# Gated linear attention and a multiplicative feed-forward on one core: masked scores in quarters, with a second load of v for the odd heads

## The chip, the cores and the metric

One core of a Trainium2 chip runs the whole program. The metric is the device time of one execution in microseconds (us); a kernel is compared by the median of its runs on the same chip. The profile is one execution, recorded by the hardware profiler.

## The reference

```python
# attention, for every one of B=4 batches and H=8 heads; S=768 tokens, D=48
state = alpha[:, :, t, :, None] * state + einsum('bhd,bhe->bhde', k[:, :, t], v[:, :, t])
y[:, :, t] = einsum('bhd,bhde->bhe', q[:, :, t], state)
# y is laid out as x: 3072 tokens x 384, then
a = x @ w1; b = x @ w2            # 384 x 1024 each
out = ((a * b) @ w3) @ w_out      # 1024 x 1024, 1024 x 384
```

Within a chunk of 128 tokens the recurrence is computed as masked attention: with q and k scaled by running products of alpha, a query t sees the keys s <= t of its chunk through a 128 x 128 matrix of scores, and everything earlier through the 48 x 48 state. Of the four 64 x 64 quarters of a score matrix one, later keys with earlier queries, is all masked.

## The kernel before, in words

**Stages.** Part 1 is a loop over N = 24 chunks (6 to a batch) of all 8 heads, into which the first gate products of the feed-forward are mixed as filler. After it come the remaining gate products, the folding of w3 with w_out, and the last projection.

**A chunk's work.** Heads go in pairs j = 0..3 with i = 0 for the even and i = 1 for the odd head; head i of a pair lies on partitions 64i to 64i+47 of `qkT`. For chunk n the pieces are:

- `load_a`, `load_kq`, `load_v`: alpha, k and q, v from memory on SP's queue, all in rows of 48 numbers (192 bytes). `load_v` (L151) writes one of four buffers `vs`.
- `logs`, `decays`, `decayed` (L288 on): Ln on ScalarE (ACT), the running sums on TensorE (L318 to L324), two Exp into a tile `e` (L326, three buffers), and the product with k and q on VectorE (DVE, L337). For every even chunk that doesn't open a batch, single rows of `e` go through memory by POOL's queue (L330, L332, L345) to become the state's decay `dec`.
- `transposed` (L348): 16 transposes into PSUM (L359), two copies to `qkT` on ACT (L361).
- `scores` (L393): 8 float32 matmuls, each of 48 rows by 128 keys as weights with 128 queries moving, the even and the odd head in two row halves of the array (L399); then two VectorE instructions that AND the 128 x 512 scores of four heads with an integer mask `keep` into the tile `ms` (L402).
- `attend_state` (L408): 8 matmuls of state with q into two PSUM banks `y`, in four 64 x 64 corners of the array (L419).
- `attend` (L422): 8 matmuls with 64 columns of v as weights and 128 columns of `ms` moving, onto the same banks (L425), in two column halves; then two copies on ACT (L429), which `store` sends to memory as `xd` (L283) one iteration later.
- `outer`, `advance`: the chunk's own k by v (L371), added to the state on VectorE (L379, L381), decayed on POOL (L390).

**The order.** Iteration n of the loop is written out by hand:

```python
store(); ...load_x, load_a(n + 5); load_kq(n + 4); load_v(n + 2)
attend_state(n - 1)
scores(n)
transposed(n + 1)
...split_x, convert
advance(n); attend(n - 1); outer(n)
...run(pieces), decayed(n + 2), logs(n + 4), decays(n + 3), convert
```

So the masks of chunk n are made in iteration n and used by `attend(n)` in iteration n+1, behind that iteration's scores and transposes. Each engine takes its instructions in one order, and SP's queue issues its DMAs in one order; a scheduler that orders a program's instructions may move one ahead of others of its engine that are not ready. The trace of before shows TensorE in the order above, and SP in it until about 140 us. From iteration 6 on `run(pieces)` adds up to three pieces of gate products (`exact`, L455), 9 matmuls of 384 columns each, to an iteration; in one iteration of four (9, 13, 17, 21) there is none. `convert` turns the float64 weights into float32 parts, mostly VectorE and ACT work, with loads `raw` of 512 KB on SP (L213).

Of the kernel before, what the change touches and what calls it, by code (L numbers as in the profile page):

```python
# [10 lines left out]
FP32 = mybir.dt.float32  # L11
FP32R = mybir.dt.float32r
I32 = mybir.dt.int32
# [3 lines left out]
ALU = mybir.AluOpType  # L17
# [31 lines left out]
def kernel(  # L49
# [12 lines left out]
    nc = tc.nc  # L62
    B, H, S, D = q.shape
    C = 128
    DM = H * D
    DF = moe_w1.shape[1]
    NCH = S // C
    N = B * NCH
    NP = H // 2
    DP = 64  # L70
# [6 lines left out]
    AHEAD = 3  # L77
    LATE = 10
    PAIRED = 8
    assert D <= DP and DM % C == 0 and DF % CW == 0 and S % C == 0 and N % G == 0  # L80
    assert DM <= 512 and TG <= 512

# [17 lines left out]
    p1 = pool("p1", 1, stack=part1, side="right", reuse_waits="tile")  # L100
# [3 lines left out]
    def bank():  # L104
        return ps.tile([C, 512], FP32, tag="bank", name="bank")

    st, mark = {}, {}
# [14 lines left out]
    vs = [p1.tile([C, H, DP], FP32, name=f"v{i}") for i in range(AHEAD + 1)]  # L122
    for x in vs:
        nc.gpsimd.memset(x[:, :, D:], 0.0)

    def rows(src, n):
        b, c = divmod(n, NCH)
        return src[b, :, ds(c * C, C), :].rearrange("h p d -> p h d")
# [22 lines left out]
    def load_v(n):  # L151
        if n < N:
            st["v", n] = vs[n % len(vs)]
            (nc.gpsimd if 2 < n < 8 else nc.sync).dma_start(out=st["v", n][:, :, 0:D], in_=rows(v, n))

    spare = tr[0].tile([C, 3 * KM * TG], FP32R, tag="x3", name="x3")[:].bitcast(FP32)
    sums2 = spare[:, 0:4 * C].rearrange("p (e s t) -> p e s t", e=2, s=2)
    pairs = [spare[:, ds(4 * C + i * 2 * DM, 2 * DM)].rearrange("p (h s d) -> p h s d", h=H, s=2) for i in range(2)]
# [18 lines left out]
    sums = p1.tile([C, 2, C], FP32R, name="sums")  # L177
    signs = p1.tile([C, 2, C], FP32R, name="signs")
    keep = p1.tile([C, C], I32, name="keep")
    qks = [p1.tile([C, 2, H, DP], FP32, name=f"qk{i}") for i in range(3)]  # L180
    Ts = [p1.tile([C, NP, DP], FP32, name=f"T{i}") for i in range(2)]
    decs = [p1.tile([C, 3, NP], FP32, name=f"dec{i}") for i in range(2)]
# [7 lines left out]

    nc.vector.tensor_scalar_mul(keep, utri, -1.0)
    keep_bc = keep[:, None, :].to_broadcast([C, NP, C])
    for x in qks:
        nc.vector.memset(x[:, :, :, D:], 0.0)
    make_identity(nc, ident)
# [115 lines left out]
    def decays(n):  # L311
        if n >= N:
            return
        lc = bank()[:, 0:DM]
        la = st.pop(("la", n))
        if paired(n):
            for i in range(2):
                nc.tensor.matmul(lc.rearrange("p (h d) -> p h d", h=H), sums2[:, n % 2, i], la[:, :, i, :],  # L318
                                 start=(i == 0), stop=(i == 1))
        elif n < LATE:  # L320
            nc.tensor.matmul(lc, sums[:, n % 2].bitcast(FP32), la, start=True, stop=True)  # L321
        else:
            for i in range(2):
                nc.tensor.matmul(lc, sums[:, n % 2], la[:, i], start=(i == 0), stop=(i == 1))  # L324

        e = st["e", n] = work.tile([C, 2, DM], FP32, tag="e", name="e", bufs=3)  # L326
        nc.scalar.activation(e[:, 0], lc, AF.Exp, scale=-1.0)  # L327
        mark["e", n] = nc.scalar.activation(e[:, 1], lc, AF.Exp).ins  # L328
        if n in ends:
            mark["pool"] = nc.gpsimd.dma_start(out=ends[n][0:1], in_=e[0:1, 0]).ins  # L330
        if n + 1 in ends:
            mark["pool"] = nc.gpsimd.dma_start(out=ends[n + 1][1:2], in_=e[C - 1:C, 1]).ins  # L332
        load_ends(n)
# [49 lines left out]
    def advance(n):  # L383

        if n not in ends:
# [4 lines left out]
        mark["pool"] = nc.gpsimd.tensor_tensor(Ts[0][:, :, 0:D], st.pop(("T", n - 1)),  # L390
                                               dec[:, :, None].to_broadcast([C, NP, D]), op=ALU.mult).ins

    def scores(n):  # L393
        qkT = st["qkT", n]
        sc = [bank().rearrange("p (j c) -> p j c", j=NP) for _ in range(2)]
        for j in range(NP):
            for i in range(2):
                r = ds(DP * i, D)
                nc.tensor.matmul(sc[i][:, j, :], qkT[r, 0, j, :], qkT[r, 1, j, :], start=True, stop=True)  # L399
        ms = work.tile([C, 2, NP, C], FP32, tag="ms", name="ms")  # L400
        for i in range(2):
            masked = nc.vector.tensor_tensor(ms[:, i].bitcast(I32), sc[i].bitcast(I32), keep_bc, op=ALU.bitwise_and)  # L402
        ends_of_part1[0] = mark["ms", n] = masked.ins
        st["ms", n] = ms

    HP = NP // 2
# [15 lines left out]
    def attend(n):  # L422
        (y, heads), ms, vc = st.pop(("y", n)), st.pop(("ms", n)), st.pop(("v", n))
        for j, i, to in heads:
            nc.tensor.matmul(to, vc[:, 2 * j + i, :], ms[:, i, j, :], start=(n % NCH == 0 and j % HP == 0),  # L425
                             stop=(j % HP == HP - 1), skip_group_check=True)
        x = work.tile([C, HP, 2, C], FP32, tag="x", name="x", bufs=4)
        for i in range(2):
            copied = nc.scalar.copy(x[:, :, i], y[i])  # L429
        ends_of_part1[1] = copied.ins  # L430
        x = x.rearrange("p j i t -> p (j i) t")

        g, c = divmod(n, G)
        to = xd[g].rearrange("(b h d) t -> b d h t", b=2, d=D)
        for half in range(2):
            later.append((to[half, :, :, ds(c * C, C)], x[ds(DP * half, D)]))
# [197 lines left out]
    for n in range(N + 1):  # L634
        store()
        if n in loads:
            load_x(loads[n])
        if n != 1 and not 2 < n <= FIRST:
            load_a(n + 5)
        raws = (3, 3, 3, 3, 2, 2, 3, 3)[n] if n < 8 else 4  # L640
        for m in (n + 3,) * (n <= FIRST) + (n + 4,) * (n >= FIRST):
            load_kq(m)
            if 2 < n <= FIRST and m == n + 3:
                load_a(n + 5)
            if n < FIRST - 2:
                fetch(raws)
        if n >= FIRST:
            load_v(n + 2)
        if n:
            attend_state(n - 1)  # L650
        if n < N:
            scores(n)
        transposed(n + 1)
        if n == 1:
            decays(3)
            load_a(6)
            with after_marks(("e", 3)):
                logs(4)
        if n == FIRST + 1:
            run(2)  # L660
        if n < FIRST:
            with after_marks("pool"):
                load_v(n + 2)
        if n - 2 in begin and n > FIRST:
            g, tiles = begin[n - 2]
            with after_marks(("ms", n), ("qkT", n + 1)):
                split_x(g, 0)
            fill.extend(gate(g, f) for f in tiles)
        if n == FIRST:
            with after_marks("l", ("qkT", n + 1)):  # L670
                split_x(0, 0)
            fill.extend(gate(0, f) for f in begin[n - 3][1])
        pieces = ((3, 3, 2, 0) if n > FIRST + 3 else (0, 3, 3, 0))[(n - FIRST) % 4] if n >= FIRST else 0
        if n == 0:
            with after_marks(("qkT", 0)):
                logs(2)
            decays(2)
            with after_marks(("e", 2)):
                logs(3)
        early, ready = n < FIRST, len(thirds) if n > 2 else n // 2  # L680
        marks = (*[("qkT", n + 1)] * (n < N - 1), *[("qk", n + 1), ("ms", n)] * early, *["x3"] * (n - 2 in begin and n > FIRST))
        if n < N - 2 and n != FIRST:
            with after_marks(*marks):
                convert(2 if early else 1, raws)
        advance(n)
        if n:
            attend(n - 1)
        outer(n)
        if n > FIRST:
            third(ready)  # L690
        run(pieces > 0)
        if early:
            with after_marks(*marks):
                convert(1, raws)
        with after_marks(*[("ms", n)] * (n < 3)):
            decayed(n + 2)
        if not early:
            with after_marks(*[("qkT", n + 1)] * (n < N - 4)):
                logs(n + 4)
        if n == 4:  # L700
            load_x(0)
        convert(early and n > 0, raws)
        run(pieces > 1)
        if n:
            decays(n + 3)
        if n <= FIRST:
            third(ready)
        if 0 < n < FIRST:
            with after_marks(("e", n + 3)):
                logs(n + 4)  # L710
        if n == FIRST:
            with after_marks("x3", ("e", n + 3)):
                convert(2, raws)
        elif n < N - 2:
            convert(n == FIRST - 1 if early else n % 3 == 0, raws)
        if n == FIRST - 1:
            assert len(done) == 2 * KM
        run(pieces > 2)
        if n == N - 3:
            while begun:  # L720
                convert(1)
            weights.extend(load_out(j) for j in range(KF))
            fetch(4)
# [91 lines left out]
```

## Time and profile before

| | before |
|---|---|
| median of 3 runs | 472.4 us (471.74 to 474.81) |
| profiled execution, its own time | 472.53 us |
| span of its instructions | 470.8 us |
| busy TensorE / VectorE / ACT / POOL | 457.6 / 358.5 / 279.1 / 80.0 us |
| memory read / written | 57.58 / 22.06 MB |
| part 1 ends (last `attend`) | about 185 us |

The page has the busy time of each engine, the span in 40 slices (11.8 us each), the DMA queues, the chain of work that ended last, the costliest groups of instructions, and the DMA issues. In the trace a float32 matmul is two records; "x16" on L399, L419 or L425 is therefore one chunk's 8 matmuls. A DMA instruction on "SPq" is SP's issue of a transfer; the data land some microseconds later. The first TensorE instruction of `scores(n)` in the trace is that of group n of L399, counted from 0; the loads of v on SP are those of chunks 0 to 2 and 8 to 23, those between are on POOL's queue.

### The profile page before, as it was taken

Reading aid. Unit: us, or ns where it says so; the run is one execution under the profiler, and the core shown is the slowest. Engines: PE = TensorE matmul, PEld = TensorE weight load, DVE = VectorE, ACT = ScalarE, POOL = GpSimd, SP = SyncE. Lnnn points to the kernel's source line nnn. Section 1 sums busy time; section 2 is a strip of 40 time slices with the busy share of each in tenths; the row PEclk is TensorE's granted clock in tenths of the full one; section 3 lists DMA queues with packets and bytes.
Section 4 is the critical chain, followed back from the end, with each engine's and each line's share of the span. In section 5 each row is a group of like instructions: output and inputs, shape, how many; then the busy total and the mean of one; then the engine's idle time right before and its main releaser. Section 6 shows DMA issues by size and latency. Waiting matters only on the chain.

```text
span 470.8 us, 10039 instructions
## 1 busy us (share of the span) xinstructions
PE 457.6 (97%) x3848; PEld 433.7 (92%) x3848; DVE 358.5 (76%) x578; ACT 279.1 (59%) x552; POOL 80.0 (17%) x149
## 2 busy tenths in 40 slices
PE   4998999999999999999999999999999999999996
PEld 2676799999989999999999999999999999999996
DVE  2788996999869797999999968764641977766671
ACT  4686866767677464889887656554553633333330
POOL 5234212023102230222221112111011000000000
PEclk9999999999999999999999999999999999999999
DMA  9999999999999853557685532212013976555511
GB/s 178 242 219 237 237 209 205 239 235 210 198 221 215 231 143 108 176 183 218 205 288 176 155 124 101 85 50 85 33 52 114 244 240 185 173 166 167 171 52 50
DMA packets 145663, 80.29 MB, mean 171 GB/s; under 512 B 96240, under 2 KB 137456, under 8 KB 145616
## 3 DMA queue, kind: packets, MB, share of 16 engines
q1 hardware_dynamic: 139840, 64.44, 56.4%
q0 software_dynamic: 5776, 15.22, 10.2%
q8 instruction: 30, 0.49, 0.5%
q14 instruction: 17, 0.14, 0.1%
HBM read 57.58 MB, written 22.06 MB: 169 GB/s over the span
## 4 chain that ended last, share of the span: by engine, by line
PE 92%; ACT 2%; DMA 2%; DVE 2%; POOL 1%; issue 1%; POOLq 0%; DVEq 0%; ACTq 0%
PE bank L455 71%; PE bank L399 5%; PE bank L425 4%; PE bank L359 3%; PE bank L419 2%; PE bank L371 2%; PE bank L557 1%; PE bank L318 1%; PE bank L324 1%; DMA dec<-ends 1%; PE bank L321 1%; DMA ends<-e 1%; DVE qk L337 0%; ACT qkT L361 0%; ACT e L327 0%
## 5 line engine op out<-in xcount | busy, mean ns | idle before, releaser
L455 PE MATMUL bank<-x,w 128*128 128x384 f32 x1152 | 212.0, 338 | 0.7 <-ACT w L256 0.5
L455 PEld LDWEIGHTS bank<-x,w 128*128 128x128 f32 x1152 | 200.2, 188 | 2.8 <-ACT w L256 0.8
L455 PE MATMUL bank<-w3o,ab 128*128 128x384 f32 x576 | 100.2, 336 | 0.0
L455 PEld LDWEIGHTS bank<-w3o,ab 128*128 128x128 f32 x576 | 99.9, 188 | 0.0
L480 ACT ACTIVATE bank<-bank 128x384 f32<-128x384 f32 x96 | 45.8, 477 | 41.5 <-PE bank L455 41.2
L464 ACT ACTIVATE t<-bank 128x384 f32<-128x384 f32 x64 | 31.4, 493 | 56.3 <-PE bank L455 55.2
L530 POOL DMA_DIRECT2D abd<-ab x45 | 26.7, 593 | 144.9 <-DVE ab L516 125.8
L516 DVE TENSOR_TENSOR ab<-bank,r 128x384 f32<-128x384 f32 x44 | 24.4, 554 | 24.6 <-ACT bank L480 15.1
L361 ACT COPY qkT<-bank 128x512 f32<-128x512 f32 x48 | 26.1, 595 | 23.2 <-PE bank L359 23.2
L586 DVE TENSOR_TENSOR ab<-abl,ab 128x1024 fp32r<-128x1024 f32 x24 | 29.4, 1224 | 12.4 <-ACT ab L585 12.4
L585 ACT ACTIVATE ab<-abl 128x1024 fp32r<-128x1024 f32 x24 | 25.5, 1061 | 20.7 <-PE bank L455 17.9
L455 PE MATMUL bank<-wo,w3T 128*128 128x384 f32 x192 | 35.9, 334 | 0.0
L455 PEld LDWEIGHTS bank<-wo,w3T 128*128 128x128 f32 x192 | 33.5, 188 | 0.0
L226 ACT ACTIVATE power<-power,rebias 128x512 uint32<-128x512 uint32 (+1 forms) x36 | 25.1, 700 | 11.7 <-DVE power L225 11.4
L337 DVE TENSOR_TENSOR qk<-kq,e 128x768 f32<-128x768 f32 x24 | 23.3, 972 | 11.4 <-ACT e L328 8.6
L402 DVE TENSOR_TENSOR ms<-bank,keep 128x512 int32<-128x512 int32 x48 | 31.1, 681 | 1.0 <-PE bank L399 0.9
L466 DVE SCALAR_TENSOR_TENSOR o<-bank,t 128x384 f32<-128x384 f32 x24 | 13.4, 557 | 23.0 <-issue 13.7
L399 PEld LDWEIGHTS bank<-qkT 48*128 48x128 f32 x384 | 24.4, 195 | 5.3 <-issue 2.8
L399 PE MATMUL bank<-qkT 48*128 48x128 f32 x384 | 29.2, 294 | 0.0
L587 DVE SCALAR_TENSOR_TENSOR ab<-ab,abl 128x1024 fp32r<-128x1024 f32 x24 | 29.2, 1218 | 0.0
L466 DVE SCALAR_TENSOR_TENSOR r<-bank,t 128x384 f32<-128x384 f32 x40 | 22.0, 552 | 8.8 <-ACT t L464 8.3
L425 PE MATMUL bank<-ms,v 128*64 128x128 f32 x384 | 27.1, 285 | 0.0
(88 smaller groups left out, 585.9 us busy)
## 6 DMA issues: line engine op xcount, KB each, us to landing
raw<-in_moe_w_dram SPq DMA_DIRECT2D x28, 512.0 KB, 5.4
abl<-abd SPq DMA_DIRECT2D x24, 512.0 KB, 4.6
abd<-ab POOLq DMA_DIRECT2D x45, 192.0 KB, 3.3
xT<-xd POOLq DMA_DIRECT2D x9, 576.0 KB, 4.5
kq<-in_k_dram SPq DMA_DIRECT2D x24, 192.0 KB, 5.2
kq<-in_q_dram SPq DMA_DIRECT2D x24, 192.0 KB, 5.8
xd<-x SPq DMA_DIRECT2D x48, 96.0 KB, 4.0
out_dram<-o SPq DMA_DIRECT2D x24, 192.0 KB, 3.5
```

Source lines behind the costliest of these rows:

```text
L361: mark["qkT", n] = nc.scalar.copy(qkT[:, :, :, ds(DP * half, DP)], tp[half]).ins
L399: nc.tensor.matmul(sc[i][:, j, :], qkT[r, 0, j, :], qkT[r, 1, j, :], start=True, stop=True)
L402: masked = nc.vector.tensor_tensor(ms[:, i].bitcast(I32), sc[i].bitcast(I32), keep_bc, op=ALU.bitwise_and)
L425: nc.tensor.matmul(to, vc[:, 2 * j + i, :], ms[:, i, j, :], start=(n % NCH == 0 and j % HP == 0), stop=(j % HP == HP - 1), skip_group_chec ...
L455: nc.tensor.matmul(p, w[part][i], x[part][i], start=start and part == parts[0] and i == 0, stop=stop and part == parts[-1] and i == n - 1, ...
L464: nc.scalar.activation(t, p1, AF.Copy, scale=(1.0 + 1.0 / P) * scale)
L466: nc.vector.scalar_tensor_tensor(to, p2, scale, t, op0=ALU.mult, op1=ALU.add)
L480: nc.scalar.activation(p, p, AF.Copy, scale=1.0 + 1.0 / P)
L530: (nc.gpsimd if late else nc.sync).dma_start(out=abd[g][:, f, :], in_=ab)
L585: nc.scalar.activation(t[:, 0], ab, AF.Copy, scale=1.0 - 2.0 ** -13)
L586: nc.vector.tensor_sub(t[:, 1], ab, t[:, 0].bitcast(FP32))
L587: nc.vector.scalar_tensor_tensor(t[:, 2], t[:, 0].bitcast(FP32), -1.0 - 1.0 / P, ab, op0=ALU.mult, op1=ALU.add)
```

## The change

From chunk 8 on (`TURNED = 8`), the score quarter of later keys and earlier queries is not computed.

- `turned_scores` takes the place of `scores`: for each head one matmul of the first 64 keys with all 128 queries, and one of the last 64 keys with the last 64 queries. The two use different column halves of the array, and for odd heads the halves are exchanged, so the four matmuls of a pair use the four corners of the array. In PSUM an odd head's first keys lie on partitions 64 to 127 and its last keys on 0 to 63.
- To match, the odd heads' v is needed with its two halves of tokens exchanged. `turn_v(n)` loads it a second time, on SP's queue, in two DMAs of 64 partitions by 4 heads by 48 numbers, into one of two new buffers `vts`. It stands in iteration n behind `load_v(n + 2)` and ahead of `attend_state`.
- The values are applied in two parts. For the first 64 queries, `attend_low` has 8 matmuls of 64 rows, 64 columns and 64 queries; those of chunk n-1 are issued two at a time between the pairs of `turned_scores(n)` (those of chunk 23 by themselves in the last iteration). For the last 64 queries, `attend` has its 8 matmuls with 64 instead of 128 moving columns.
- The mask takes four VectorE instructions in place of two, each of 4 x 64 elements a partition; `keep_turned` is the odd heads' mask, made at the start on POOL (two copies and a memset). POOL also zeroes the padding of `vts` at the start.
- The tile `e` has two buffers in place of three.

```diff
+    TURNED = 8
+    vts = [p1.tile([C, NP, DP], FP32, name=f"vt{i}") for i in range(2)]
+    for x in vts:
+        nc.gpsimd.memset(x[:, :, D:], 0.0)
...
+    def turn_v(n):
+        if turned(n):
+            for half in range(2):
+                nc.sync.dma_start(out=vts[n % 2][ds(DP * half, DP), :, 0:D],
+                                  in_=rows(v, n)[DP * (1 - half):DP * (2 - half), 1::2])
...
+    for half in range(2):
+        nc.gpsimd.tensor_copy(out=keep_turned[ds(DP * half, DP), 1 - half], in_=keep[ds(DP * half, DP), ds(DP * half, DP)])
+    nc.gpsimd.memset(keep_turned[DP:, 1], -1)
...
-        e = st["e", n] = work.tile([C, 2, DM], FP32, tag="e", name="e", bufs=3)
+        e = st["e", n] = work.tile([C, 2, DM], FP32, tag="e", name="e", bufs=2)
...
+    def attend_low(n, jj, i, half):
+        s, w = ds(DP * i, DP), (vts[n % 2] if i else st["v", n])
+        h = half * NP // 2 + jj
+        nc.tensor.matmul(st["y", n][0][i][ds(DP * half, DP), jj, 0:DP], w[s, h if i else 2 * h, :],
+                         st["ms", n][s, i, h, 0:DP], start=(n % NCH == 0 and jj == 0), stop=True, skip_group_check=True)
+    def turned_scores(n):
+        qkT = st["qkT", n]
+        sc = [bank().rearrange("p (j c) -> p j c", j=NP) for _ in range(2)]
+        for j in range(NP):
+            for part in range(2):
+                for i in range(2):
+                    r, t = ds(DP * i, D), slice(DP * part, C)
+                    nc.tensor.matmul(sc[i][ds(DP * (part ^ i), DP), j, t], qkT[r, 0, j, ds(DP * part, DP)],
+                                     qkT[r, 1, j, t], start=True, stop=True)
+            if turned(n - 1):
+                for i in range(2):
+                    attend_low(n - 1, j % 2, i, i ^ (j < 2))
+        ms = work.tile([C, 2, NP, C], FP32, tag="ms", name="ms")
+        for i in range(2):
+            r = ds(DP * i, DP)
+            low, high = (keep_turned[r, 0], keep_turned[:, 1]) if i else (keep[r, 0:DP], keep[:, DP:])
+            for x, mask, t in ((slice(DP * i, DP * (i + 1)), low, slice(0, DP)), (slice(0, C), high, slice(DP, C))):
+                masked = nc.vector.tensor_tensor(ms[x, i, :, t].bitcast(I32), sc[i][x, :, t].bitcast(I32),
+                                                 mask[:, None, :].to_broadcast([x.stop - x.start, NP, DP]),
+                                                 op=ALU.bitwise_and)
...
     def scores(n):
+        if turned(n):
+            return turned_scores(n)
...
         for j, i, to in heads:
-            nc.tensor.matmul(to, vc[:, 2 * j + i, :], ms[:, i, j, :], start=(n % NCH == 0 and j % HP == 0),
-                             stop=(j % HP == HP - 1), skip_group_check=True)
+            if turned(n):
+                w = vts[n % 2][:, j, :] if i else vc[:, 2 * j, :]
+                nc.tensor.matmul(to[:, DP:], w, ms[:, i, j, DP:], start=False,
+                                 stop=(j % HP == HP - 1), skip_group_check=True)
+            else:
+                nc.tensor.matmul(to, vc[:, 2 * j + i, :], ms[:, i, j, :], start=(n % NCH == 0 and j % HP == 0),
+                                 stop=(j % HP == HP - 1), skip_group_check=True)
...
         if n >= FIRST:
             load_v(n + 2)
+        turn_v(n)
         if n:
             attend_state(n - 1)
         if n < N:
             scores(n)
+        else:
+            for j in range(NP):
+                for i in range(2):
+                    attend_low(n - 1, j % 2, i, i ^ (j < 2))
         transposed(n + 1)
```

More of the change, by code (lines that the diff above doesn't have):

```diff
@@ L154, in load_v, with turned @@
             (nc.gpsimd if 2 < n < 8 else nc.sync).dma_start(out=st["v", n][:, :, 0:D], in_=rows(v, n))
+    def turned(n):
+        return TURNED <= n < N
+    def turn_v(n):
[3 more added lines that the diff above has]
+                                  in_=rows(v, n)[DP * (1 - half):DP * (2 - half), 1::2])
     spare = tr[0].tile([C, 3 * KM * TG], FP32R, tag="x3", name="x3")[:].bitcast(FP32)
@@ L179 @@
     keep = p1.tile([C, C], I32, name="keep")
+    keep_turned = p1.tile([C, 2, DP], I32, name="keep_turned")
     qks = [p1.tile([C, 2, H, DP], FP32, name=f"qk{i}") for i in range(3)]
@@ L391, in advance @@
                                                dec[:, :, None].to_broadcast([C, NP, D]), op=ALU.mult).ins
+    def attend_low(n, jj, i, half):
[23 more added lines that the diff above has]
+                                                 op=ALU.bitwise_and)
+        ends_of_part1[0] = mark["ms", n] = masked.ins
+        st["ms", n] = ms
     def scores(n):
+        if turned(n):
+            return turned_scores(n)
         qkT = st["qkT", n]
```

## The prediction

> **What bounds the kernel now.** First the page's busy times and slices (11.8 us each), then its groups, for what the change touches.
>
> ```profile
> PE   4998999999999999999999999999999999999996
> ...
> DMA  9999999999999853557685532212013976555511
> ...
> L399 PE MATMUL bank<-qkT 48*128 48x128 f32 x384 | 29.2, 294 | 0.0
> ...
> L425 PE MATMUL bank<-ms,v 128*64 128x128 f32 x384 | 27.1, 285 | 0.0
> ```
>
> TensorE is busy 97% of the span, but the DMA engines are full as well for the first 14 slices, to about 165 us, and the changed chunks 8 to 23 run from 68 to 185 us. The second view, the chain of waits in order of time (start, us, what), gives the real length of each piece, as overlaps are taken out there:
>
> ```profile
> 90.39 0.60 PE bank L419 x16
> 90.98 1.09 PE bank L399 x16
> 92.08 0.49 PE bank L359 x16
> 92.57 1.02 PE bank L425 x16
> ...
> 102.13 0.45 PE bank L371 x16
> ```
>
> So a chunk pays 1.09 us for scores and 1.02 for values. Third, the timeline where the changed scores of chunk 9 begin (start, us, engine, line):
>
> ```profile
> 77.48 1.16 PE L399 MATMUL bank<-qkT 48*128 48x128 f32 x16
> ...
> 77.69 1.03 SPq L154 DMA_DIRECT2D v<-in_v_dram  x1
> ...
> 78.76 1.00 SPq L213 DMA_DIRECT2D raw<-in_moe_w_dram  x1
> ```
>
> The load at 77.69 is v of chunk 10 (SP's loads are chunks 0, 1, 2, 8, 9, 10...), issued in SP's iteration 8, while TensorE begins iteration 9. SP, whose issues follow one another with hardly a gap from 66 to 162 us, is an iteration behind. Loads of kq, v and alpha are made two or more iterations ahead, so the lag shows nowhere now. Of v's landing, that line's view says:
>
> ```profile
> DMA to landing us min/median/max: 3.4/5.0/7.1
> ```
>
> **What the skill says.** The Trainium skill, "TensorE: Matmul & The Clock Gate", Part 2: matmuls stay in program order and only weight loads are pulled ahead, so one that waits for its load stops all behind it; the trace agrees where TensorE sat until 44.00 us for POOL's T with scores queued behind. Part 1 of that page: after about 3.4 us of idleness the array runs at half rate for as long again. The chain agrees:
>
> ```profile
> 43.35 0.60 POOL T L390
> 44.00 0.67 PE bank L419 x16
> 44.67 1.39 PE bank L399 x16
> ```
>
> After that stall scores took 1.39 instead of 1.09 us. The page "TensorEngine Tiling (Array Packing)", Key Properties: tiles work independently, and a change of tiling drains the array. The trace shows equal tiles side by side: state's 8 matmuls in four corners take 0.60 us where 8 of the same 128 columns in two halves take 1.02 to 1.09. Unequal ones it doesn't show. "DMA: Bandwidth & Descriptors", Issuing engines are not separate DMA queues: all queues share the same 16 engines; so more loads delay every other one, which the full DMA row bears out.
>
> **The change, part by part.**
>
> *TensorE, scores and low values.* Two matmuls side by side are a round. Scores are 8 rounds of 128 columns (both records counted) in 1.09 us, state 4 in 0.60: about 0.12 a round and 0.11 for the start. Transposes are 8 rounds of 64 columns in 0.49, outer 8 of 48 in 0.45: 0.06 a round of 64. Now a pair has, in four corners, two matmuls of 128 columns, two of 64, and two low ones of 64. For j = 0, 1 the low ones follow on the corners of the short ones: 2 rounds of 128, 0.24 us. For j = 2, 3 they follow on the corners of the long ones: 0.24 + 0.12 = 0.36. Sum 2 x 0.24 + 2 x 0.36 + 0.11 = 1.31, against 1.09: +0.22. If unequal matmuls don't run side by side, a pair is 0.24 + 0.12 + 0.12 = 0.48, the sum 2.03: +0.94. It can't be under the long corner's own 1.2, so +0.1 is the lower end.
>
> *TensorE, values.* 8 rounds of 64 instead of 128 columns: about 0.52 (transposes 0.49, outer 0.45) instead of 1.02: -0.50, at worst -0.3. The net is -0.25 us a chunk (taken: corners do run independently for state), from -0.4 to +0.6; over 16 chunks -4, from -6 to +10. The last low part, alone in iteration 24, costs some 0.35 once, which that iteration's shorter values give back.
>
> *VectorE.* Two masks of 512 elements at 0.68 us become four of 256. The rows of 192 and 384 elements (0.35 and 0.55) give 1.05 ns an element; 256 is 0.42, four are 1.67 against 1.36: +0.3 a chunk, 5 us in all. VectorE is busy 102.9 of the 120 us from 66 to 186, which covers it on the whole; from 106.2 to 118.8 it is busy 12.50 of 12.60, and there and in two stretches like it, about half the chunks, 0.3 each would show: 2.5 us if nothing else made TensorE wait. Beside the waits below I count 0.
>
> *SP's queue and the DMA engines.* Two loads a chunk, 49 KB each in 192-byte rows. Issue: about 0.45 us each, like ac (0.41) and half the xd pair (0.86). Transfer: at the some 220 GB/s that the page has for these slices, 98 KB are 0.45 us a chunk on engines already full. What stands behind them on SP, that iteration's raw and ab and all of the next, moves back by as much, and by more each chunk: 4.5 us after ten chunks.
>
> *The wait.* This is the step I expect to decide. Attend_low of chunk 8 stands behind the first four matmuls of scores(9), 0.2 us after 77.48, so at 77.7. Its load stands behind v of chunk 10, which is issued at 77.69 and leaves SP at 78.72: even the issue comes a microsecond too late. Behind v's median landing of 5.0 us: 77.69 + 5.0 + 0.45 = 83.1 (81.5 by the fastest landing). TensorE waits 5.4 us, and scores, transposes, values and gates are queued behind. Next, chunk 9: v of chunk 11 is issued at 86.23, now 0.45 later, so the turned load lands at 86.7 + 5.0 + 0.45 = 92.1 (90.5 by the fastest). TensorE, shifted by 5.4 and some 1 us of half rate, wants it at 81.69 + 0.2 + 6.4 = 88.3: 3.8 more (2.2). The shift is then about 10 us, an iteration's length, and TensorE no longer leads SP. Check at chunk 18: v of chunk 19 is issued at 141.77, now after nine pairs, 4.0 later; landing 3.4 to 5.0 and 0.45 on top: 149.6 to 151.2, wanted at 139.44 + 0.2: a shift of 10.0 to 11.6 whatever TensorE saved before. I take 10.5. From chunk 18 on SP has fewer loads (alpha and kq end) and the savings count: 6 x 0.25 = 1.5. Net +9.
>
> *At nothing.* `e` in two buffers: Exp of e(n+2) now waits for qk(n) and the copy of single rows of e(n); qk(12) for example begins at 88.95, Exp of e(14) at 97.8. Only e(5) at 30.2 is close; without that cover up to 1 us. The start on POOL: some five instructions of 0.1 to 0.3 us; TensorE's first matmul at 4.53 needs the sums (ready at 3.56) and the Ln (4.38), so 0.8 us of cover; without it under 1 us.
>
> *Sum.* 472.53 for the profiled execution (span 470.8 and 1.7 around it), which is the median's 472.4 within 0.1: 472.4 + 10.5 - 1.5 = 481.4.
>
> **Rivals.**
> (a) *The waits are covered*, and it isn't slower. Place: SP's order and TensorE's order in iterations 8 to 10. A scheduler may put the turned loads ahead of kq and v, or other matmuls ahead of the low ones. For: SP's trace shows such moves late (kq at 142.26 ahead of xd at 144.12). Against: no such move in SP's trace before 140 us, and none on TensorE. Price: the saving of 4 us stays, 468.4, less up to 4 for VectorE and DMA. It decides if the load for chunk 8 is issued before 77.7 - 5.0 = 72.7 us, ahead of that iteration's alpha at 73.85, and so on in each.
> (b) *Unequal matmuls don't pack*, so TensorE pays up to +0.6 a chunk on top of the wait; six chunks after the 18th and some before: 481.4 + 1.5 + 4 to 6 = 488. For: no row shows unequal ones. Without the waits it would give 472.4 + 10 = 482, so the profile must tell it from my case by the length of scores.
> (c) *VectorE is the bound*: 472.4 - 4 + 5 = 473 with no wait on DMA. For: 99% busy from 106 to 119. Against: TensorE's own pieces have no gaps there.
> (d) The change does nothing: not possible from chunk 8 on, as nothing else computes there.
>
> **How the numbers follow.** My case 0.63 (its own range 476.5 to 487.5); (a) with (c) 0.25 (467 to 477), of which a fifth under 467.7; (b) 0.12 (483 to 492). About 1% is what a measurement tells from no change: 467.7 to 477.1. Faster 0.05, from (a); the same 0.20, the rest of (a) and (c) and the low end of mine; slower 0.75. The time is 481.4; the range 473 to 488.5 leaves out half of (a) and (c) and the top of (b), some 0.18.
>
> **What would show it.** TensorE idle some 5 us from about 77.7, released by the DMA into vt, and a few us more at chunk 10; later short waits of the same kind, most in the short iterations; scores 1.3 us and values 0.5; masks about 0.42; the loads of v, kq and alpha landing later by up to 4 us. If low parts find their load in place, or scores take 2 us, I am wrong in the step named there.

## The result and the profile after

The changed kernel takes 488.88 us in the median of its 4 runs (484.81 to 491.91), the kernel before 473.51 in the runs beside it: a ratio of 1.0325, 95% interval 1.0287 to 1.0364. It is slower, as forecast, but by 15.4 us where 9 were forecast, and just beyond the upper end of the range. The profiled execution is the slowest of the four: 491.91 us, with a span of 490.2.

The page of the changed kernel, same rows as before, with the row of the clock that TensorE was granted:

```profile
PE   4998996996999999999999999999999999999996
...
PEclk9999998897699999999999999999999999999999
DMA  9999999989888977357668442122101886556511
```

Two holes in TensorE's row, in slices 7 and 10 (from about 74 and 110 us), each with a lower clock in it and behind it. In the profile of before every digit of the clock is 9. Behind slice 15 TensorE's two rows are those of before: the loss lies in part 1. Its last `attend` ends 18.3 us later than before, of 19.4 us that the span has grown.

The first hole in the chain of waits (start, us, what):

```profile
77.43 0.69 PE bank L376 x16
78.12 0.11 SPq L158
78.23 0.04 issue
78.27 2.42 SPq L166
80.69 0.04 issue
80.74 2.40 DMA vt<-in_v_dram
83.14 0.04 issue
83.18 0.70 PE bank L414 x8
```

L158 is the load of v of chunk 10, L166 the second load of v of chunk 8, L414 the low values. The load is issued behind v of chunk 10 and lands at 83.14; the forecast had 83.1. The odd heads' four low matmuls (x8, two records each) come together behind the transposes (L376), the even heads' values and most of `outer`, not between the scores (L425): their order on TensorE isn't that of the program, so the wait lies there. TensorE stands still for 4.28 us from 78.9. The second hole:

```profile
114.45 0.41 PE bank L477 x8
114.86 0.32 SPq L166
115.18 0.05 issue
115.23 3.36 DMA vt<-in_v_dram
118.59 0.14 issue
118.72 0.70 PE bank L414 x8
```

The load is the fifth pair of L166, issued from 114.42 on behind v of chunk 14. So the hole belongs to chunk 12, in iteration 13; the forecast had the second wait at chunk 9, in iteration 10. The two add up in the list of waits (us in all, times, longest):

```profile
PE bank L414 <- DMA vt<-in_v_dram: 8.2, 2, 4.3
```

A last gap of 1.08 us at 187.69, for which the profile names nothing, makes 9.25. What comes behind each hole shows in the busy times by stretch (stretch and its length; PE, PEld, DVE, ACT, POOL busy; clock; DMA share; GB/s):

```profile
82.86:89.69 6.83, 6.51 (x92) 5.72 (x92) 4.96 (x8) 2.80 (x6) 2.02 (x2) 0.50 1.11 252
89.70:117.00 27.30, 25.13 (x378) 22.83 (x374) 24.21 (x50) 15.83 (x36) 3.99 (x8) 1.00 0.95 192
117.00:130.65 13.65, 11.93 (x153) 10.87 (x154) 6.65 (x11) 6.28 (x13) 2.43 (x4) 0.50 0.99 203
```

For 6.83 and again for 13.65 us TensorE runs at half clock, and it is busy there but for the end of each hole. The kernel before has one such period, of 3.4 us at 45.3. In the chain one sees it in the pieces: state with q, 0.60 us at full clock, takes 1.06, and eight records of gate products 2.58, or 322 ns each, where 18 take 3.32 at full clock, or 184 each:

```profile
105.80 0.60 PE bank L469 x16
...
108.96 3.32 PE bank L510 x18
...
122.86 1.06 PE bank L469 x16
...
128.53 2.58 PE bank L510 x8
```

Measured at the start of each chunk's transposes, the changed kernel is 1.1 us ahead at chunk 10, 6.1 behind at 11, 7.0 at 13, 12.1 at 14, 17.0 at 16, 17.7 at 18 and 19.4 at 20. So it moves by steps, at the two holes and the half clock behind each: from chunk 10 to 13 it loses 8.1 us, of which 4.28 are the wait, and from 13 to 16 another 10.0, of which 3.89 are.

### The profile page after: what moved, and what is told of

Same layout as the page of the kernel before. It is cut to its first block, busy times and chain, and to the rows that moved or that the text cites. A ratio compares the mean times of both kernels' runs of the same rounds, so it can differ in the third digit from the quotient of the medians.

```text
span 490.2 us, 11155 instructions
## 1 busy us (share of the span) xinstructions
PE 466.9 (95%) x4360; PEld 441.7 (90%) x4360; DVE 363.7 (74%) x610; ACT 280.3 (57%) x552; POOL 78.9 (16%) x154
## 4 chain that ended last, share of the span: by engine, by line
PE 88%; DMA 4%; DVE 4%; ACT 2%; issue 1%; SPq 1%; DVEq 0%; ACTq 0%
PE bank L510 68%; PE bank L425 3%; PE bank L376 3%; PE bank L477 2%; PE bank L469 2%; PE bank L388 2%; PE bank L414 2%; PE bank L612 1%; PE bank L341 1%; PE bank L335 1%; DMA abl<-abd 1%; DMA vt<-in_v_dram 1%; DMA kq<-in_q_dram 1%; DVE ms L452 1%; PE bank L338 1%
## 5 line engine op out<-in xcount | busy, mean ns | idle before, releaser
L585 POOL DMA_DIRECT2D abd<-ab x45 | 25.7, 570 | 146.2 <-DVE ab L571 127.8
L245 DVE SCALAR_TENSOR_TENSOR mant<-mant,rest 128x512 f32<-128x512 uint32 (+1 forms) x36 | 23.9, 664 | 2.8 <-ACT rest L238 2.7
L238 ACT ACTIVATE rest<-raw 128x512 f32<-128x512 uint32 (+1 forms) x36 | 23.3, 650 | 1.4 <-DMA raw<-in_moe_w_dram 1.4
L376 PE MATMUL bank<-ident,qk 64*128 64x64 f32 x384 | 20.1, 247 | 3.8 <-DVE qk L354 2.2
L246 DVE SCALAR_TENSOR_TENSOR power<-raw,power 128x512 uint32<-128x512 uint32 (+1 forms) x36 | 23.3, 654 | 0.3 <-ACT power L243 0.2
```

Of the source, the lines that this page charges most:

```text
L376: nc.tensor.transpose(tp[half][:, i, j, :], qk[s, i, 2 * j:2 * j + 2, :], ident[s, s])
L585: (nc.gpsimd if late else nc.sync).dma_start(out=abd[g][:, f, :], in_=ab)
```

## The experiments

### The quarters without the second load

```diff
-        turn_v(n)
-                w = vts[n % 2][:, j, :] if i else vc[:, 2 * j, :]
+                w = vc[:, 2 * j + i, :]
```

(and the same in `attend_low`).

> Changed kernel without the second load: the odd heads' parts take v as it is loaded for the even heads, so their values are of the wrong keys; the instructions of all compute engines are the same. It shows what the quarters cost by themselves. Theory A: 469 to 474 us, with scores 0.2 us longer and values 0.5 us shorter a chunk. Rival B: 480 or more. Rival C doesn't tell it from A.

Measured: 471.76 us, ratio 0.9958 (0.9940 to 0.9977). There is no wait for vt, and the clock is halved for 3.4 us only. So the quarters themselves gain 2 us, and the whole loss, some 17 us, comes with the second load.

### The load an iteration earlier

```diff
-        turn_v(n)
...
             attend(n - 1)
+        turn_v(n + 1)
         outer(n)
```

> Changed kernel, with the second load of v for chunk n+1 issued on SP in iteration n behind attend(n - 1), an iteration earlier than in the changed kernel; all else as there. Theory A (the waits of TensorE for that load, and the half clock rate behind them, are the whole loss): no wait of several us, clock full from 68 us on, 471 to 477 us. Rival B (the quartered matmuls themselves cost more, or don't pack): 483 or more. Rival C (the added transfers on full DMA engines delay the other loads): 480 or more.

Measured: 484.43 us, ratio 1.0251 (1.0197 to 1.0306). The wait for vt of chunk 8, now issued at 68.9, is gone. TensorE waits 2.5 us for that of chunk 9 instead, in iteration 10, where the forecast for the changed kernel had its second wait: it is issued at 79.3, behind v of chunk 10 and a load of weights, and lands at 85.2. The wait for chunk 12 is gone too, but TensorE waits 1.8 us for v itself at 147.8. An earlier place in the program brings little: the queue is behind.

### Only the second load, read by nobody

The kernel before, with `turn_v`, `vts` and two buffers for `e`.

```diff
+        turn_v(n)
         if n:
             attend_state(n - 1)
```

> Kernel before, with the second load of v issued as in the changed kernel but read by nobody, and e in two buffers. Theory A: within 1.5 us of before, as the lag of SP's queue shows only where somebody waits for the new load. Rival C: 5 to 10 us slower, with waits of TensorE for v or VectorE for kq.

Measured: 480.6 us, ratio 1.0161 (1.0128 to 1.0195). That is a miss for the theory, which had only waits for vt in mind. The chain near 144 us shows what is late:

```profile
144.28 0.01 PE bank L367
144.29 4.15 DMA v<-in_v_dram
148.44 0.14 issue
148.58 0.67 PE bank L379 x16
```

L379 is `outer`, which needs v of chunk 18. Nothing here reads the second load; v came late since SP issued it late. SP's row for that v, in the timeline of the kernel before:

```profile
135.23 0.70 SPq L154 DMA_DIRECT2D v<-in_v_dram  x1
```

and of this one, with the pair behind it:

```profile
144.29 0.74 SPq L156 DMA_DIRECT2D v<-in_v_dram  x1
145.08 1.31 SPq L161 DMA_DIRECT2D vt<-in_v_dram  x2
```

From v of chunk 10 to v of chunk 18 SP takes 66.8 us in place of 57.5, and eight pairs lie between: 1.15 us a pair. (The kernel before with two buffers for `e`, as this one has, takes 59.3; against it a pair is 0.94.) Some 1.5 us of this kernel's loss are already there at chunk 9, in front of the added loads, where the kernels with nothing added until then stand between 1.3 us ahead and 3.2 behind.

### A quarter of the bytes, the same number of issues

```diff
-                nc.sync.dma_start(out=vts[n % 2][ds(DP * half, DP), :, 0:D],
-                                  in_=rows(v, n)[DP * (1 - half):DP * (2 - half), 1::2])
+                nc.sync.dma_start(out=vts[n % 2][ds(DP * half, DP), 0:1, 0:D],
+                                  in_=rows(v, n)[DP * (1 - half):DP * (2 - half), 1:2])
```

> The kernel before plus the unread loads on SP's queue (64 partitions each), with one head of 48 numbers in place of four: a quarter of the bytes and rows, the same number of issues. The full unread loads cost 7 us and moved v of chunk 18 back by 9.1 us on SP's queue; on POOL's queue, with the values in use, by 6.1. Theory A' (the issues themselves take SP's time): v of chunk 18 still some 5 us or more behind, 477 us or more. Rival C' (bytes and rows on the DMA engines, which hold SP's issues back): v of chunk 18 no more than 3 us behind, no wait for v, 473 to 475 us.

Measured: 479.28 us, ratio 1.0124 (1.0092 to 1.0156), and the same v is as late as with four times the bytes:

```profile
145.42 0.81 SPq L156 DMA_DIRECT2D v<-in_v_dram  x1
146.28 1.36 SPq L161 DMA_DIRECT2D vt<-in_v_dram  x2
```

From chunk 10's v to chunk 18's: 67.6 us, 1.26 a pair (1.04 against 59.3). A quarter of the bytes takes nothing off, so on SP the cost is that of the issue, some 0.6 us each. The time of this kernel is not a clean measure of it: 3.2 us of its profile's loss are there at chunk 9, before the added loads count, with a load of kq of 8.05 us in the chain.

### The load on POOL's queue, at its place and an iteration earlier

```diff
-                nc.sync.dma_start(out=vts[n % 2][ds(DP * half, DP), :, 0:D],
+                nc.gpsimd.dma_start(out=vts[n % 2][ds(DP * half, DP), :, 0:D],
```

> The changed kernel with the second load of v issued on POOL's queue instead of SP's, at the same place of the program. SP's queue then has nothing new, but POOL's queue is in order behind its own copies and waits. Theory A' (the load comes late because it stands behind other loads on SP's queue, and v comes late because the pair of issues takes over 1.2 us of that queue in each iteration; the half-clock periods follow from these waits): no wait of TensorE for v, and waits for vt gone or under 1 us in all, 471 to 477 us. Rival C' (the DMA engines' own transfers are the cost, whoever issues): waits for v or vt of several us remain, 480 us or more. Rival P (POOL's own work holds the issue back): waits for vt of some us in the iterations in which POOL is late, none for v, 477 to 486 us.

Measured: 481.13 us, ratio 1.0165 (1.0128 to 1.0202). There is no wait for v. From chunk 9 to chunk 18 the shift stays between 1.5 and 2.3 us: POOL's pairs cost TensorE nothing there. (The pairs for chunks 8 and 9, whose buffers are free from the start, go out at 8.4 to 10.9 us, when POOL's queue has time.) Late in part 1 the load stands behind POOL's copies of `dec` (L362), which wait for theirs:

```profile
167.87 1.42 POOL dec L362 x2
169.29 0.62 POOL vt L166
169.91 5.33 DMA vt<-in_v_dram
175.23 0.04 issue
175.28 0.37 PE bank L414
```

So rival P's mechanism is there, beside a part of A', and the time is in P's range. SP, without the pairs, takes 63.7 us from chunk 10's v to chunk 18's, against 59.7 in the kernel without the load: 0.5 us a pair, though no issue was added to its queue. The Trainium skill's page "DMA: Bandwidth & Descriptors", Issuing engines are not separate DMA queues, states that transfers run on the same 16 DMA engines and interleave whichever engine starts them; this is in keeping with it. But a quarter of the bytes on SP's queue took nothing off, so what the transfers cost by themselves isn't settled.

> As the run with POOL's queue, and the load of chunk n+1's second v is issued in iteration n, one iteration (some 10 us) earlier. Theory A': no wait of TensorE for vt or v at all, no half-clock period beyond those of the kernel before, and the quarters' own gain of some 2 us as in the run without the second load: 470 to 474 us. Rival C' (the transfers themselves): 478 us or more, with waits for v. Rival P (POOL's queue is held back by more than an iteration): 474 to 480 us.

Measured: 479.57 us, ratio 1.0115 (1.0080 to 1.0149), above what A' gave and within P's range. At chunk 9 it is 6 us behind, with a gap of 4.7 us at 43 us. It waits for vt 1.6 us at 154 and 3.5 at 175; a gap of 1.2 us at 89 is one for which the profile names nothing. With two buffers the load for chunk 10 is held until the values of chunk 8 are done: it is issued at 86.1.

> The kernel before plus the second load of v, read by nobody, on POOL's queue (e in two buffers to make room, as in the change). On SP's queue the same addition cost 7 us. Theory A' (it was SP's queue): within 2 us of before, no waits for v. Rival C' (it was the DMA engines): 5 us or more above before, with waits for v near 112 and 146 us as on SP's queue.

Measured: 490.47 us, ratio 1.0355 (1.0328 to 1.0382), where neither theory looked. As nobody reads the loads, all 32 are issued from 7 to 64 us, ahead of POOL's other work; the loss of 19.5 us is complete at chunk 9, and from there to chunk 23 the shift changes by 0.2. So this run tells nothing of loads at their place, only that a load without a reader doesn't stay there on POOL.

### Two buffers for `e` alone

```diff
-        e = st["e", n] = work.tile([C, 2, DM], FP32, tag="e", name="e", bufs=3)
+        e = st["e", n] = work.tile([C, 2, DM], FP32, tag="e", name="e", bufs=2)
```

> The kernel before with e in two buffers instead of three, and nothing else. My prediction counted nothing for this, at most 1 us: within 1 us of before. Rival E (the missing buffer delays the Exp or decays in the early chunks, where two of the variants had PE gaps near 41 us): 2 us or more slower, with a gap of TensorE near 41 us.

Measured: ratio 0.9992 (0.9970 to 1.0013). Nothing, as the forecast had it.

### Filling the waits with matmuls

24 dense matmuls behind the scores of iterations 9 and 14 of the changed kernel, to keep TensorE busy.

```diff
+        if n in (9, 14):
+            p = bank()[:, 0:TG]
+            for i in range(24):
+                nc.tensor.matmul(p, sums[:, 0], w12[0][:, 0, 0, 0, 0:TG], start=(i == 0), stop=(i == 23))
```

> Changed kernel with 24 extra dense matmuls of 128 x 384, read by nobody, in TensorE's order behind the scores of chunks 9 and 14, where it waits for the second load; 9 us more work for TensorE. Theory A with the half clock as its larger part (8 us of the loss): the waits become shorter by as much as the added work, the clock stays full, 479 to 485 us, faster than the changed kernel's 488.9. Rival (the clock doesn't matter, the waits alone do): 489 or more, and if TensorE isn't idle there as the trace says, 498.

Measured: 490.94 us, ratio 1.0392 (1.0337 to 1.0448). Only the first wait was filled: the second one of the changed kernel is in iteration 13, so the second filler (122.5 us) comes behind it. At the first, the wait fell from 4.28 to 1.09 us and the half clock behind it went; from chunk 9 to 11 the shift grows by 6.0 us, filler included, in place of 7.3. But half clock came at 116.7 (10.2 us), behind a wait of 1.39 us in iteration 13, and at 161.1 (6.8 us), behind one of 2.67. As a whole this is inconclusive.

### Exchange on the chip in place of the load

```diff
-                nc.sync.dma_start(out=vts[n % 2][ds(DP * half, DP), :, 0:D],
-                                  in_=rows(v, n)[DP * (1 - half):DP * (2 - half), 1::2])
+                nc.gpsimd.tensor_copy(out=vts[n % 2][ds(DP * half, DP), :, 0:D],
+                                      in_=st["v", n][ds(DP * (1 - half), DP), 1::2, 0:D])
```

called behind `outer(n)`; the other version has `nc.scalar.copy`.

> The changed kernel in which the second load of v is replaced by two copies on ACT from v's own buffer, partitions 64-127 to 0-63 and 0-63 to 64-127, behind the outer products of iteration n. No DMA is added. If the whole loss comes from the second load (its place and time on SP's queue and its transfer), the time falls to that of the run without the load, 470 to 473.5 us, scores and values in program order, no wait for vt over 0.5 us. If ACT becomes what TensorE waits for (two copies of some 0.4 us a chunk on an engine that is in order and busy 279 us), 474 to 479. If the split matmuls themselves were the loss, 480 or more.

Measured on ACT: 473.26 us, ratio 1.0002 (0.9985 to 1.0019).

> As the run with copies on ACT, with the copies on POOL, which is busy only 80 us. If POOL takes them between its waits: 470 to 473.5 us. If POOL's own in-order waits for the decay rows hold the copies back by some us (as they held back the loads on its queue in chunks 19 to 22): waits of TensorE for vt, 474 to 480 us.

Measured on POOL: 472.08 us, ratio 0.9981 (0.9965 to 0.9998). A copy takes 366 ns in the median, and the low values stand between the scores, as written. This does the same work as the changed kernel without its loss, and is the quickest version with right values, by 0.2% only. Its pieces at chunk 11 answer to those of the kernel before at 90.39:

```profile
91.42 0.60 PE bank L468 x16
92.02 0.16 PE bank L424 x5
...
93.12 0.64 PE bank L375 x16
93.77 0.61 PE bank L476 x16
94.38 1.78 PE bank L509 x9
```

From state to the end of the values it is 94.38 - 91.42 = 2.96 us, before 93.59 - 90.39 = 3.20: -0.24, where the forecast had -0.25.

### The two waits alone

The version with copies on POOL, with one more write to v of chunk 8 (its padding) behind the first low matmul, and its copies made six times over.

```diff
                 for i in range(2):
                     attend_low(n - 1, j % 2, i, i ^ (j < 2))
+                    if j == i == 0 and n - 1 in (8,):
+                        nc.gpsimd.memset(st["v", n - 1][0:DP, 4, D:], 0.0)
+                        for _ in range(6):
+                            turn_v(n - 1)
```

> The kernel with the copies on POOL and no second load (472.1 us), in which the odd heads' low matmuls of chunk 8 are held for some 4.5 us: the padding of v of chunk 8 is zeroed again on POOL once the first even low matmul has read it, and the two copies of 0.36 us each are made six times over behind that. Nothing else is late, no DMA is added. It puts the changed kernel's first wait, 4.3 us near 79 us, into a kernel without its other troubles. Theory H (the wait is paid twice, as TensorE then runs at half clock in two periods of 3.4 us): 479 to 481.5 us, with a half-clock period some 4 us after the gap begins. Rival W (only the wait itself counts, the half clock in the changed kernel has another cause): 476 to 477.5 us. Rival S (slack behind TensorE takes part of it): under 475.5 us.

Measured: 479.05 us, 7.0 more than without the hold (ratio to before 1.0109, 1.0077 to 1.0142). The hold came about otherwise than meant: POOL made the copies early, at 65 to 74 us, but the write to v (L430) stood behind POOL's own wait for the decay rows until 85.5, and the values of chunk 8 (L480), which read v, waited for it. In the timeline that wait of TensorE is 5.81 us (in brackets):

```profile
85.70 0.37 PE L480 MATMUL bank<-ms,v 128*64 128x64 f32 x1 [5.81 <-POOL v L430]
```

and behind it the clock is halved, with TensorE busy, for the same 6.83 us as in the changed kernel:

```profile
79.89:84.67 4.78, 0.00 (x1) 0.00 (x0) 0.81 (x2) 2.46 (x4) 0.60 (x2) 1.00 0.93 237
84.67:91.50 6.83, 5.80 (x96) 5.27 (x96) 3.83 (x6) 2.35 (x6) 3.08 (x7) 0.50 0.93 220
91.50:101.50 10.00, 10.00 (x179) 9.40 (x175) 9.21 (x19) 6.41 (x14) 1.72 (x3) 1.00 1.00 204
```

Without the hold there is a gap of 1.23 us nearby, so the wait is 4.6 us more; 7.0 - 4.6 = 2.4 us for 6.8 at half clock, 0.35 a us.

The other version has `n - 1 in (8, 13)`; its second hold is one chunk behind the changed kernel's second wait.

> As the run before with a second such hold, at chunk 13, the place of the changed kernel's second wait (3.9 us near 115 us, half clock for 13.7 us after it). Theory H: 486 to 490 us, as slow as the changed kernel, and then the two waits with their half-clock periods explain its whole loss. Rival W: 480 to 482 us. Rival S: under 479 us.

Measured: 484.71 us, 12.6 more than without holds (ratio to before 1.0239, 1.0199 to 1.0279), in neither range. The shift is counted here from the version without holds. At the first hold TensorE waits 6.49 us, 5.3 more than without it, and the shift grows by 7.1, with 6.83 us at half clock: 0.27 a us. The second hold came out shorter than meant, 1.19 us at 117.9 and 0.98 at 121.7, and yet the clock is halved from 120.0 for 6.83 us and the shift goes from 6.2 to 11.2: 5.0 us for 2.2 of waiting, 0.41 us for each us at half clock. So in these three holds a wait costs 1.3 to 2.3 times its length, with the half clock behind it. That is theory H's mechanism; its range for two holds was for a longer second one.

## Why the prediction was wrong, point by point

- **The first wait** was right in place and cause. That its landing fits (83.14 for 83.1) is luck: the forecast had 0.45 us for an issue and 5.0 us from the issue of v to the landing. Measured, the first of the two issues alone took 2.42 us, and the data landed 2.40 us behind the start of the second. TensorE waited 4.28 us, not 5.4, as other matmuls ran ahead of the odd heads' low ones.
- **The second wait** was misplaced. The forecast took TensorE's order as written. In iterations 9 to 14 of the changed kernel the odd heads' low matmuls run 6 to 9 us behind the even heads'; in 10, 11, 12 and 14 gate products run ahead of them, which hides the load. Iterations 9 and 13 have no gate products, and these two have the waits, so the forecast's sign "most in the short iterations" came true. In the versions that issue on POOL's queue, or copy, the low matmuls mostly stand as written. The order came from the scheduler; why it chose so was not tried.
- **SP's queue**, "about 0.45 us each" and 0.45 for the transfer: the forecast then let only one 0.45 a chunk count, "4.0 later" for chunk 19's v after nine pairs. Measured are 0.94 to 1.15 and, with a quarter of the bytes, 1.04 to 1.26 us a pair. The issues follow one another on a full queue, and their own length (624 ns in the median in the changed kernel) is what counts. This term was too small by half or more, and so v itself came late where the load had no reader or stood an iteration earlier, which was not forecast.
- **"Some 1 us of half rate"** is the step that failed most. The mechanism was named, its size was not right. By the three holds a us at half clock costs 0.27 to 0.41 us; the changed kernel has 20.5 us of it in part 1, 17.1 more than before: 4.6 to 7.0 us. With 9.25 us of waits that is 13.9 to 16.3 of the 18.3 us of part 1 in the profile; the rest is not told apart by a run. A part of it may be odd heads' low matmuls by themselves, eight records in 0.39 us at full and 0.70 at half clock. The forecast reasoned with 3.4 us of idleness and read the stall before 45.3 us as agreeing. TensorE had stood still there for only 0.32 and 0.93 us, so the trace of before already showed the half clock behind short gaps.
- **"A shift of 10.0 to 11.6 whatever TensorE saved before"** at chunk 18 took TensorE to be held by SP from then on. Measured are 17.7. The v of chunk 19 is issued 12.5 us later than before (154.25 for 141.77), and no wait for vt is left there: the two holes and the half clock set the shift, not SP.
- **The saving.** The sum of TensorE's pieces at chunk 11 is right to 0.01 us, but not its parts as the chain has them: scores with low values take 1.10 us (forecast 1.31), the transposes, which the forecast left alone, 0.64 in place of 0.49, the values 0.61 (forecast 0.52). So a part of that fit is luck. In the total, chunks 12 to 23 gain 0.15 us each in the kernel without the load and 0.09 with copies on POOL. In the stretch from 106.2 to 118.8 us TensorE is busy 12.59 of 12.60 us in the former, so what is missing there doesn't show as waiting; in the latter it is busy 12.35, with VectorE at 12.47 (12.50 before). In the changed kernel nothing is gained from chunk 18 to 23: it loses 0.7 us more, where the forecast had a gain of 1.5. One gap of 1.0 to 1.2 us near 83.5 in both versions comes on top; the profile names nothing that it waits for.
- **At nothing**: `e` in two buffers cost nothing, as forecast.
- **The rivals.** (a) half came: the scheduler did move matmuls, which postponed the second wait and didn't remove it. (b) is refuted by the pieces: unequal matmuls in four corners do run side by side (1.10 us for scores with low values, not 2.03). (c) can have a small part at most: TensorE waits 0.2 us for masks near 111 us in the version with copies on POOL, and 0.6 near 172 in it and in the kernel without the load; no run took the masks away.

## What to carry to other kernels

On a queue whose issues follow one another without a gap, price a new transfer at the length of its issue, once for each transfer: here a quarter of the bytes made it no cheaper. It adds up, and what comes late in the end may be an old load. Price a wait of TensorE amid small matmuls above its own length, as the slower clock behind it counts too: here 1.3 to 2.3 times. Look for the wait where the order of the trace puts it, in the iterations with no other work to run ahead. Where the data are on the chip already, copy them there, on an engine with time to spare.

## What the runs showed of the hardware

- The Trainium skill's page "TensorE: Matmul & The Clock Gate", Part 1, has an idle window of about 3.4 us as what halves the clock and a busy one of that length as what restores it. Here the half clock came in periods of 3.41 us or multiples, 6.83 us behind a wait of 4.28 or 5.81 and 13.65 behind one of 3.89. It came behind shorter gaps as well: in the 3.4 us ahead of it TensorE stood still for 1.25 us in the kernel before (at 45.3) and for 1.42 in the version with two holds (at 120.0; 0.23 and 1.19). A gap of 1.23 us in the version with copies on POOL brought none. What decides it, and what makes it two periods or four, stays open.
- A DMA of 64 partitions took SP 624 ns to issue (median) with 256 rows of 192 bytes and 600 ns with 64.
- Copies of 64 partitions by 192 numbers onto the other 64 partitions took 366 ns on POOL in the median and 351 ns on ACT in the mean.
